# A decode step with attention and a gated MLP on one core: TensorE's middle as a loop, K transposed as 32-bit words, thin products with the activations stationary

## The chip, the cores and the metric

The kernel runs on one core of a Trainium2 chip. The metric is device time in microseconds, median of several executions. A profile of one execution stands beside the times; its span runs from the first to the last instruction and is a little shorter than the device time.

## The reference

```python
def reference(A_x, A_k_cache, A_v_cache, A_wq, A_wo, B_x, B_W_gate, B_W_up, B_W_down, gate_w):
    # x (4,1,512); caches (4,8,16384,128), the last W = 4096 rows count; 32 query heads, 4 per kv head
    q = (x @ wq) as (4, 32, 1, 128)
    p = softmax(q k^T * 128**-0.5);  o = p v
    a = o as (4, 1, 4096) @ wo
    gate = x @ W_gate;  up = x @ W_up                # 512 -> 1792
    b = (gate * (gate > 0) * up) @ W_down            # 1792 -> 512
    g = sigmoid((x * gate_w).sum(-1))
    return g * a + (1 - g) * b                       # x = A_x for both
```

All tensors are bf16. With 4 rows of activations the work is to bring in 81 MB: K and V 33.5 MB each, wq and wo 4.2 MB each, gate, up and down 1.8 MB each.

## The kernel before, in words

The 4 x 8 kv heads are taken four at a time, as eight **sets** `s` (`NSET`): one batch element and one half of its kv heads. A set's K is one 4 MB transfer into one half of `Ksb` (`load_k`, L158), its V the same into `Vsb` (`load_v`, L162); the two halves take turns. All big transfers are issued on SP's queue in one order: wq, K0, K1, V0, K2, V1, ..., K7, V6, gate, up, V7, down, wo in three pieces (`WO_CUTS`, L182). K of set `s` may be overwritten when the scores of `s` are done, V when its values are done. W_gate and W_up go into the first half of `Ksb`, W_down into that of `Vsb`, wo over wq in `Wbig`.

A list `Program` holds each engine's operations in an order written out by hand; `emit` turns named events into semaphore waits. Everything is unrolled. The phases of a set:

- `kt(s, i)`, i = 0..15 (L258): eight 128 x 128 bf16 transposes on PE (the piece of K stationary, `ident` moving) into one of three PSUM banks; one copy back into the same place of `Ksb`, nine on ACT (L263, `ACT_TAKES`), seven on DVE (L265).
- `scores(s, m)`, m = 0..7 (L280): four matmuls with `qT` stationary, side by side in four column groups of the array, 512 columns of transposed K moving; every second m a DVE instruction adds `mask` and takes the maximum (L290).
- `maximum`, `exponent`, `turn` (L297 to L326): the maximum over a head's keys, exp on ACT with row sums, a DVE transpose of the probabilities into `pT`.
- `values(s, k)`, k = 0..3 (L338): sixteen matmuls with `pT` stationary (32 columns), 256 columns of V moving, in four column groups; then a copy `osb`.
- `combine(s)` (L351, L354): eight fp32 matmuls with the selector `Wsel`, one with `Wsum`, a reciprocal and a product into `oq`.

PE's order interleaves transposes and scores of set `s` with the values of `s-1` and the combine of `s-2`. Ahead of set 0 stand the transpose of x (L226, fp32), the sigmoid gate and `qproj` (L366: 128 pairs, wq stationary, 4 columns of x moving). Behind set 7 stand `gateup` (L379: 112 pairs with W stationary, its columns read with a step of 14), the last values and combine, the down product (L444, 56 pairs) and wo (L452, 128 pairs), all with the weights stationary and 4 columns moving, into 16 columns of one bank; then a copy, a PE transpose, a copy and the output's transfer (L456 to L461).

Of the kernel before, what the change touches and what calls it, by code (L numbers as in the profile page):

```python
# [13 lines left out]
HQ = 32  # L14
# [5 lines left out]
NSET = 8  # L20
NFT = FF // 128
SCALE = DH ** -0.5
# [3 lines left out]
NTR = 3  # L26
NSC = 3
NPIECE = 2
NBANK = 4
WO_CUTS = (0, 16, 28, 32)  # L30
ACT_TAKES = (0, 1, 4, 6, 8, 9, 11, 13, 14)


class Program:

# [3 lines left out]
    def __init__(self):  # L39
        self.ops = {e: [] for e in self.ENGINES}  # L40
        self.events = {}
        self.counts = {e: 0 for e in self.ENGINES}
        self.dmas = []

    def op(self, engine, fn, name=None, waits=()):
        if name is not None:
            assert name not in self.events, name
            self.counts[engine] += 1
            self.events[name] = (engine, self.counts[engine])
        self.ops[engine].append((fn, name, tuple(waits), False))  # L50

    def dma(self, engine, fn, name, waits=()):
        assert name not in self.events, name
        sem = "d%d" % len(self.dmas)
        self.dmas.append(sem)
        self.events[name] = (sem, 16)
        self.ops[engine].append((fn, name, tuple(waits), True))

    def emit(self, engine, eng, sems):
        seen = {}  # L60
        for fn, name, waits, is_dma in self.ops[engine]:
            need = {}
            for w in waits:
                if w is None:
                    continue
                s, n = self.events[w]
                need[s] = max(need.get(s, 0), n)
            for s, n in need.items():
                if seen.get(s, 0) < n:
                    eng.wait_ge(sems[s], n)  # L70
                    seen[s] = n
            if fn is None:
                continue
            ins = fn(eng)
            if name is not None:
                s, _ = self.events[name]
                ins.then_inc(sems[s], 16 if is_dma else 1)


def bass_gated_mix__sliding_block_cached__glu_gated_reglu__decode_kernel(  # L80
# [13 lines left out]
    with ExitStack() as ctx:  # L94
# [7 lines left out]
        pT = sb("pT", [128, 2, 2048], BF16)  # L102
        mask = sb("mask", [128, 512], BF16)
        ident = sb("ident", [128, 128], BF16)
        ones = sb("ones", [128, 128], BF16)
# [6 lines left out]
        xT = sb("xT", [128, 32], BF16)  # L112
        xw = sb("xw", [5, 512], FP32)
        identf = sb("identf", [5, 8], FP32)
        gwB = sb("gwB", [128, 512], BF16)
        gsb = sb("gsb", [128, 8], FP32)
        qT = sb("qT", [128, NSET, 48], BF16)
# [12 lines left out]
        gtmp = sb("gtmp", [128, NFT * 4], FP32)  # L130
        gtmp2 = sb("gtmp2", [128, NFT * 4], FP32)
        hT = sb("hT", [128, NFT * 4], BF16)
        outT = sb("outT", [128, 16], BF16)
        out16 = sb("out16", [16, 128], BF16)
# [5 lines left out]

        Wg = Ksb[:, 0, 0:4 * FF].rearrange("p (t f) -> p t f", t=4)
# [7 lines left out]
        def trb(f):  # L149
            return TR[f % NTR][:].bitcast(BF16)  # L150

# [5 lines left out]
        def load_k(s):  # L157
            P.dma("sp", lambda e: e.dma_start(Ksb[:, s % 2, :], heads(A_k_cache, s)), ("K", s),  # L158
                  [("SC", s - 2, 2 * NBANK - 1)] if s >= 2 else [])

        def load_v(s):
            P.dma("sp", lambda e: e.dma_start(Vsb[:, s % 2, :], heads(A_v_cache, s)), ("V", s),  # L162
                  [("PV", s - 2, 3)] if s >= 2 else [])
# [3 lines left out]
        P.dma("sp", lambda e: e.dma_start(Wbig[:, :], A_wq.rearrange("(p t) w -> p (t w)", p=128)), ("WQ",))  # L167
        load_k(0)
        for s in range(1, NSET):
# [3 lines left out]
              ("WG",), [("SC", NSET - 2, 2 * NBANK - 1)])  # L173
        P.dma("sp", lambda e: e.dma_start(Ksb[:, 0, 4 * FF:8 * FF], B_W_up.rearrange("(p t) f -> p (t f)", p=128)),
              ("WU",), [("SC", NSET - 2, 2 * NBANK - 1)])
# [9 lines left out]
        P.op("pool", lambda e: e.memset(ones[:, :], 1.0), ("ONES",))  # L185
        P.op("pool", lambda e: e.affine_select(ident[:, :], ones[:, :], [[-1, 128]], ALU.is_equal, 0.0,
                                               base=0, channel_multiplier=1), ("IDENT",), [("ONES",)])
        P.op("pool", lambda e: e.memset(onesf[:, :], 1.0), ("ONESF",))
        P.op("pool", lambda e: e.memset(m4[:, :], -NEG), ("M4Z",))
        for a in range(4):  # L190
# [21 lines left out]
        P.op("dve", lambda e: e.memset(qT[:, :, :].rearrange("p s w -> p (s w)"), 0.0), ("QZ",))  # L212
# [4 lines left out]
        P.op("pool", lambda e: e.affine_select(identf[:, :], onesf[0:5, 0:8], [[-1, 8]], ALU.is_equal, 0.0,  # L217
                                               base=0, channel_multiplier=1), ("IDENTF",), [("ONESF",)])
        P.op("dve", lambda e: e.memset(xw[:, :], 0.0), ("XW0",))
        xwv = xw[:, :].bitcast(BF16).rearrange("r (k h) -> r k h", h=2)  # L220
        P.op("dve", lambda e: e.tensor_copy(xwv[:, :, 0:1], xsb[:, :].rearrange("r (k h) -> r k h", h=1)),  # L221
             ("XW",), [("XW0",), ("X",), ("GW",)])
        xv = xw[:, :].rearrange("r (p t) -> r t p", t=4)
        fbf = FB[:].bitcast(BF16).rearrange("p (k h) -> p k h", h=2)
        for t in range(4):
            P.op("pe", lambda e, t=t: e.transpose(FB[:, t * 8:t * 8 + 5], xv[0:5, t, :], identf[0:5, 0:5]),  # L226
                 ("XT",) if t == 3 else None, [("XW",), ("IDENTF",)])
        P.op("dve", lambda e: e.tensor_copy(xT[:, :].rearrange("p (t r) -> p t r", t=4)[:, :, 0:5],
                                            fbf[:, 0:32, 0].rearrange("p (t r) -> p t r", t=4)[:, :, 0:5]),
             ("XTC",), [("XT",)])  # L230
        P.op("dve", lambda e: e.tensor_copy(gwB[:, :].rearrange("p (t m) -> p t m", t=4),
                                            xT[:, :].rearrange("p (t r) -> p t r", t=4)[:, :, 4:5].to_broadcast([128, 4, 128])),
             ("GWB",), [("XTC",)])
        for t in range(4):
            P.op("pe", lambda e, t=t: e.matmul(FB[:, 32:36], gwB[:, t * 128:(t + 1) * 128], xT[:, t * 8:t * 8 + 4],
                                               start=(t == 0), stop=(t == 3)),
                 ("Z",) if t == 3 else None, [("GWB",)])
        P.op("act", lambda e: e.activation(gsb[:, 0:4], FB[:, 32:36], ACTF.Sigmoid), None, [("Z",)])
        P.op("act", lambda e: e.activation(gsb[:, 4:8], FB[:, 32:36], ACTF.Sigmoid, scale=-1.0), ("G",))
# [3 lines left out]
        tr_of = {}  # L243
# [4 lines left out]
        def kt(s, i):  # L248
            f = len(fills)
            fills.append((s, i))  # L250
            tr_of[(s, i)] = f
            bk = trb(f)
            for cc in range(8):
                c = 8 * i + cc
                w = []
                if cc == 0:
                    w = [("K", s), ("IDENT",)] + ([copy_done(f - NTR)] if f >= NTR else [])
                P.op("pe", lambda e, bk=bk, cc=cc, c=c, s=s: e.transpose(  # L258
                    bk[:, cc * 128:(cc + 1) * 128], Ksb[:, s % 2, c * 128:(c + 1) * 128], ident[:, :]),
                    ("KT", s, i) if cc == 7 else None, w)  # L260
            dst = Ksb[:, s % 2, i * 1024:(i + 1) * 1024]
            if i in ACT_TAKES:
                P.op("act", lambda e: e.activation(dst, bk[:, :], ACTF.Copy), ("KTC", s, i), [("KT", s, i)])  # L263
            else:
                P.op("dve", lambda e: e.tensor_copy(dst, bk[:, :]), ("KTC", s, i), [("KT", s, i)])  # L265

        def scores(s, m):
            bank, e2 = m // 2, m % 2
# [3 lines left out]
            lo = 16 * (1 - e2)  # L272
            k3 = Ksb[:, s % 2, :].rearrange("p (c k) -> p c k", k=128)
            for a in range(4):
                w = []
                if a == 0:
                    w = [("KTC", s, 2 * m), ("KTC", s, 2 * m + 1), ("QC",)]
                    if prev >= 0:
                        w.append(("SCC", prev // NBANK, prev % NBANK))
                P.op("pe", lambda e, a=a: e.matmul(  # L280
                    bk[32 * a:32 * a + 32, 0:512], qT[:, s, lo:lo + 32],
                    k3[:, 16 * m:16 * m + 16, 32 * a:32 * a + 32], start=(e2 == 0), stop=(e2 == 1),
                    tile_position=(0, 32 * a)),
                    ("SC", s, m) if a == 3 else None, w)
            if e2 == 0:
                return
            w = [("SC", s, m), ("MASK",)]
            if s >= 2 and bank == 0:
# [3 lines left out]
                mx[:, s % 2, bank:bank + 1]), ("SCC", s, bank), w)  # L292
# [31 lines left out]
        def turn(s, k):  # L324
            par = s % 2
            P.op("dve", lambda e: e.transpose(pT[:, par, k * PW:(k + 1) * PW], sc[:, par, k * PW:(k + 1) * PW]),  # L326
                 ("PTT", s, k), [("EXP", s, k), ("PV", s - 2, 3) if s >= 2 else None])

        def values(s, k):
            par = s % 2  # L330
            v4 = Vsb[:, par, :].rearrange("p (k g c d) -> p k c g d", k=4, g=2, d=128)
            for c in range(16):
                g = c % 4
                w = []
                if c == 0:
                    w = [("PTT", s, k * NPIECE // 4), ("V", s), ("OSB", s - 1) if s >= 1 else None]
                col = (16 * k + c) * 32
                P.op("pe", lambda e, c=c, g=g, col=col: e.matmul(  # L338
                    OB[32 * g:32 * g + 32, 0:256], pT[:, par, col:col + 32], v4[:, k, c, :, :],
                    start=(k == 0 and c < 4), stop=(k == 3 and c >= 12), tile_position=(0, 32 * g)),  # L340
                    ("PV", s, k) if c == 15 else None, w)
            if k == 3:
                P.op("dve", lambda e: e.tensor_copy(osb[:, par, :], OB[:, 0:256]), ("OSB", s),  # L343
                     [("PV", s, 3), ("SUMS", s - 2) if s >= 2 else None])

        def combine(s):
            par, b, half = s % 2, s // 2, s % 2
            r = slice(64 * half, 64 * half + 64)
            for k in range(8):
                lo = 3 - k % 4 + 64 * (k // 4)  # L350
                P.op("pe", lambda e, k=k, lo=lo: e.matmul(FB[r, 256:288], Wsel[:, lo:lo + 64], osb[:, par, 32 * k:32 * k + 32],  # L351
                                                          start=(k == 0), stop=(k == 7)), None,
                     [("OSB", s), ("WSUM",), ("QC",), ("G",), ("OQ", s - 1) if s >= 1 else None, ("H",) if s == NSET - 1 else None])
            P.op("pe", lambda e: e.matmul(FB[r, 288:288 + NPIECE], Wsum[:, :], rowsum[:, par, :], start=True, stop=True),  # L354
                 ("SUMS", s), [("EXP", s, NPIECE - 1)])
# [157 lines left out]
```

## Time and profile before

| | |
|---|---|
| device time, median of 3 runs | 200.47 us (200.23 to 200.69) |
| the profiled execution | span 198.9 us; of its device time nothing but this span is given |
| PE, PEld busy | 140.3 us, 110.7 us (2369 instructions each) |
| DVE, ACT, POOL busy | 101.5, 91.7, 5.5 us |
| read from HBM | 81.01 MB, mean 407 GB/s over the span |
| mean granted TensorE clock | 0.882 |

PE is the row of matmuls, PEld that of weight loads, which run beside them. Shares of busy time are averages over stages; the slices of the page, the windows and the timeline show a stage by itself. "L258" is line 258 of the kernel before.

### The profile page before, as it was taken

What the parts mean: (1) busy time and instruction counts of PE and PEld (TensorE: products, weight loads), DVE (VectorE), ACT (ScalarE), POOL (GpSimd) and SP (SyncE); (2) the same over time, 40 slices, a digit from 0 to 9 for tenths busy, and PEclk for the clock granted to TensorE, in tenths of its full rate; (3) what the DMA queues carried; (4) which work ended last, traced back from release to release, by engine and by line L of the source; (5) the groups of instructions that cost most, each with busy time, mean ns of one, the idle gap of its engine ahead of it and who ended that gap; (6) DMA issues with size and microseconds to landing.
All of it is one profiled execution on the core that took longest, in us unless ns stands there. A gap on an engine that the chain in (4) does not pass through costs nothing.

```text
span 198.9 us, 5220 instructions
## 1 busy us (share of the span) xinstructions
PE 140.3 (71%) x2369; PEld 110.7 (56%) x2369; DVE 101.5 (51%) x277; ACT 91.7 (46%) x108; POOL 5.5 (3%) x29
## 2 busy tenths in 40 slices
PE   0143199879789739983995299939994998179834
PEld 0133198547576438753773286738764865178733
DVE  1200034998688526854885168456845785611200
ACT  2000059698398318842972088507851883400000
POOL 7300000000000000000000000000000000000000
PEclk9999999999999957999999669975997899855755
DMA  6999999999999999999999999999999999999960
GB/s 225 435 442 458 435 428 422 419 422 420 445 435 432 428 432 430 432 428 419 422 425 435 438 435 428 420 428 425 428 432 435 419 406 437 459 398 419 419 258 7
DMA packets 3375, 81.33 MB, mean 409 GB/s; under 512 B 405, under 2 KB 410, under 8 KB 538
## 3 DMA queue, kind: packets, MB, share of 16 engines
q1 hardware_dynamic: 3344, 81.01, 95.4%
q8 instruction: 18, 0.29, 0.6%
q14 instruction: 3, 0.02, 0.0%
q10 hardware_dynamic: 10, 0.01, 0.0%
HBM read 81.01 MB, written 0.00 MB: 407 GB/s over the span
## 4 chain that ended last, share of the span: by engine, by line
DMA 59%; PE 30%; ACT 8%; issue 1%; SPq 1%; DVE 0%
DMA Ksb<-in_A_k_cache_dram 46%; PE bank L258 19%; DMA Wbig<-in_A_wo_dram 13%; ACT Ksb L263 6%; PE bank L280 6%; PE bank L338 3%; PE bank L351 2%; ACT sc L319 1%; PE bank L452 1%; ACT L319 1%; SPq L182 0%; SPq L167 0%; SPq L177 0%; PE bank L459 0%; PE bank L354 0%
## 5 line engine op out<-in xcount | busy, mean ns | idle before, releaser
L263 ACT ACTIVATE Ksb<-bank 128x1024 bf16<-128x1024 bf16 x72 | 71.0, 1023 | 67.8 <-PE bank L258 67.8
L258 PE MATMUL bank<-ident,Ksb 128*128 128x128 bf16 x1024 | 78.6, 238 | 30.2 <-DMA Ksb<-in_A_k_cache_dram 28.0
L258 PEld LDWEIGHTS bank<-ident,Ksb 128*128 128x128 bf16 x1024 | 66.9, 108 | 45.6 <-DMA Ksb<-in_A_k_cache_dram 29.8
L265 DVE COPY Ksb<-bank 128x1024 bf16<-128x1024 bf16 x56 | 38.2, 686 | 48.2 <-PE bank L258 47.9
L280 PE MATMUL bank<-Ksb,qT 128*32 128x512 bf16 x256 | 25.1, 398 | 3.5 <-ACT Ksb L263 2.4
L290 DVE CUSTOM_DVE_ANT_0 sc<-bank,mask 128x512 bf16<-128x512 f32 x32 | 21.5, 679 | 4.9 <-PE bank L280 4.1
L326 DVE STREAM_TRANSPOSE pT<-sc 128x1024 bf16<-128x1024 bf16 x16 | 19.7, 1234 | 2.9 <-ACT sc L319 2.9
L338 PE MATMUL bank<-Vsb,pT 128*32 128x256 bf16 x512 | 20.8, 291 | 0.0
L319 ACT ACTIVATE sc<-sc,negmax 128x1024 bf16<-128x1024 bf16 x16 | 18.3, 1144 | 4.6 <-DVE negmax L311 4.6
L338 PEld LDWEIGHTS bank<-Vsb,pT 128*32 128x32 bf16 x512 | 13.8, 102 | 3.8
L280 PEld LDWEIGHTS bank<-Ksb,qT 128*32 128x32 bf16 x256 | 6.6, 93 | 11.9 <-ACT Ksb L263 3.9
L379 PE MATMUL bank<-xT,Ksb 128*128 128x4 bf16 x112 | 6.9, 199 | 5.3 <-DVE oq L359 5.3
L351 PE MATMUL bank<-osb,Wsel 128*64 128x32 f32 x128 | 9.0, 225 | 1.2 <-DVE mq L297 0.7
L379 PEld LDWEIGHTS bank<-xT,Ksb 128*128 128x128 bf16 x112 | 6.8, 158 | 5.3 <-issue 5.3
L351 PEld LDWEIGHTS bank<-osb,Wsel 128*64 128x64 f32 x128 | 8.1, 139 | 2.7 <-DVE osb L343 1.0
L226 PE MATMUL bank<-identf,xw 5*128 5x5 f32 x4 | 0.6, 262 | 8.6 <-DVE xw L221 8.6
L452 PE MATMUL bank<-oq,Wbig 128*128 128x4 bf16 x128 | 3.7, 168 | 3.7 <-DMA Wbig<-in_A_wo_dram 3.7
L452 PEld LDWEIGHTS bank<-oq,Wbig 128*128 128x128 bf16 x128 | 3.6, 103 | 3.9 <-DMA Wbig<-in_A_wo_dram 3.9
L366 PE MATMUL bank<-xT,Wbig 128*128 128x4 bf16 x128 | 3.6, 166 | 2.9 <-DMA Wbig<-in_A_wq_dram 2.9
L226 PEld LDWEIGHTS bank<-identf,xw 5*128 5x128 f32 x4 | 0.6, 207 | 8.6 <-DVE xw L221 8.6
L311 DVE TENSOR_SCALAR negmax<-mall 32x1 f32<-32x1 f32 x32 | 4.6, 144 | 1.0
L366 PEld LDWEIGHTS bank<-xT,Wbig 128*128 128x128 bf16 x128 | 3.5, 104 | 3.0 <-DMA Wbig<-in_A_wq_dram 3.0
(53 smaller groups left out, 44.2 us busy)
## 6 DMA issues: line engine op xcount, KB each, us to landing
Ksb<-in_A_k_cache_dram SPq DMA_DIRECT2D x8, 4096.0 KB, 23.7
Vsb<-in_A_v_cache_dram SPq DMA_DIRECT2D x8, 4096.0 KB, 32.8
Wbig<-in_A_wq_dram SPq DMA_DIRECT2D x1, 4096.0 KB, 12.3
Wbig<-in_A_wo_dram SPq DMA_DIRECT2D x1, 2048.0 KB, 22.4
Ksb<-in_B_W_gate_dram SPq DMA_DIRECT2D x1, 1792.0 KB, 17.0
Ksb<-in_B_W_up_dram SPq DMA_DIRECT2D x1, 1792.0 KB, 20.9
Vsb<-in_B_W_down_dram SPq DMA_DIRECT2D x1, 1792.0 KB, 16.5
Wbig<-in_A_wo_dram SPq DMA_DIRECT2D x1, 1536.0 KB, 25.6
```

The lines of the kernel that those rows point to most:

```text
L258: P.op("pe", lambda e, bk=bk, cc=cc, c=c, s=s: e.transpose(bk[:, cc * 128:(cc + 1) * 128], Ksb[:, s % 2, c * 128:(c + 1) * 128], ident[:, :]),
L263: P.op("act", lambda e: e.activation(dst, bk[:, :], ACTF.Copy), ("KTC", s, i), [("KT", s, i)])
L265: P.op("dve", lambda e: e.tensor_copy(dst, bk[:, :]), ("KTC", s, i), [("KT", s, i)])
L280: P.op("pe", lambda e, a=a: e.matmul(bk[32 * a:32 * a + 32, 0:512], qT[:, s, lo:lo + 32], k3[:, 16 * m:16 * m + 16, 32 * a:32 * a + 32], s ...
L290: P.op("dve", lambda e: e.tensor_tensor_reduce(sc[:, s % 2, bank * 512:(bank + 1) * 512], bk[:, :], mask[:, :], 1.0, LOWEST, ALU.add, ALU.max,
L319: P.op("act", lambda e: e.activation(sc[:, par, k * PW:(k + 1) * PW], sc[:, par, k * PW:(k + 1) * PW], ACTF.Exp, bias=negmax[:, par:par + ...
L326: P.op("dve", lambda e: e.transpose(pT[:, par, k * PW:(k + 1) * PW], sc[:, par, k * PW:(k + 1) * PW]), ("PTT", s, k), [("EXP", s, k), ("PV ...
L338: P.op("pe", lambda e, c=c, g=g, col=col: e.matmul(OB[32 * g:32 * g + 32, 0:256], pT[:, par, col:col + 32], v4[:, k, c, :, :], start=(k == ...
L351: P.op("pe", lambda e, k=k, lo=lo: e.matmul(FB[r, 256:288], Wsel[:, lo:lo + 64], osb[:, par, 32 * k:32 * k + 32], start=(k == 0), stop=(k ...
L366: P.op("pe", lambda e, h=h, t=t: e.matmul(FB[:, 64 + 4 * h:68 + 4 * h], Wq3[:, t, 128 * h:128 * h + 128], xT[:, t * 8:t * 8 + 4], start=(t ...
L379: P.op("pe", lambda e, W=W, i=i, t=t, col=col: e.matmul(FB[:, col:col + 4], W[:, t, i:i + NFT * 127 + 1:NFT], xT[:, t * 8:t * 8 + 4], star ...
L452: P.op("pe", lambda e, i=i, cb=cb, last=last: e.matmul(AB[:, 4 * cb:4 * cb + 4], Wo3[:, i, cb * 128:(cb + 1) * 128], oq3[:, :, i], start=F ...
```

## The change

- **A loop on PE.** PE's operations of sets 2 to 7 are emitted once, as a loop of three turns with two sets each. `turn_edge` marks the edges, `signature` sees that all turns are alike. At the end of a turn PE drains and lowers the semaphores on which it waits within the turn, so that the next turn waits for the same counts. For this DVE, ACT and POOL count towards PE on semaphores of their own (`vd`, `va`, `pq`), K and V on one for each half, and `qS` holds a set's q in a place that depends on the set's parity alone. The other engines stay unrolled.
- **K as 32-bit words.** A transpose moves 128 x 128 words of two bf16 (`Kw`, `identw`): 64 instead of 128 a set, 16 copies of 512 words. Transposed K then has two neighbouring elements of the head beside each other; `scores` reads every second one (index `o`) against q ordered in the same way (`qW`). There are four transpose banks instead of three, two score banks instead of three.
- **Activations stationary.** q, gate and up take `xT` (32 columns, four used) as stationary operand and 512 or 448 columns of weights as moving, four column groups side by side; q is then copied and transposed with 16 small matmuls, the hidden row with a DVE transpose. down and wo take `hT` and `oq` (4 columns) as stationary, 128 columns moving in each of four column groups, and the sum stands in four rows of one bank, which two copies each on DVE and ACT take to `outr`.
- **wo's pieces** are rows 0 to 25, 26 to 29, and rows 30 and 31 in two halves of 256 columns; ahead of rows 0 to 25, of rows 26 to 29 and of the first half, four matmuls whose result is not used (`warm`) are emitted.
- **Ends.** wq's transfer is issued ahead of the block, the wait for the output's stands behind it.

```diff
-NTR = 3
-NSC = 3
+NTR = 4
+NSC = 2
-WO_CUTS = (0, 16, 28, 32)
+WO_CUTS = (0, 26, 30)
+LOOP_FIRST = 2
+LOOP_TURNS = 3
...
+        t = self.turns
+        self.emit_list(eng, sems, engine, ops[:t[0]], {}, {})
...
+        with eng.Fori(0, len(t) - 1):
+            self.emit_list(eng, sems, engine, ops[t[0]:t[1]], {}, {})
+            eng.drain()
+            for s, n in self.lowered.items():
+                eng.sem_inc(sems[s], -n)
+        shift = {s: (len(t) - 1) * n for s, n in self.lowered.items() if s not in self.shared}
+        self.emit_list(eng, sems, engine, ops[t[-1]:], shift, {})
...
+        Kw = Ksb[:, :, :].rearrange("p s w -> p (s w)").bitcast(FP32).rearrange("p (s w) -> p s w", s=2)
...
-        P.dma("sp", lambda e: e.dma_start(Wbig[:, :], A_wq.rearrange("(p t) w -> p (t w)", p=128)), ("WQ",))
...
+        wo_src3 = A_wo.rearrange("(p i) w -> p i w", p=128)
+        for u in range(2):
+            P.dma("sp", lambda e, u=u: e.dma_start(Wo3[:, WO_CUTS[-1]:32, 256 * u:256 * u + 256],
+                                                   wo_src3[:, WO_CUTS[-1]:32, 256 * u:256 * u + 256]), ("WOL", u), [("Q",)])
...
+        for half in range(2):
+            for t in range(4):
+                for g in range(4):
+                    col = 512 * (4 * half + g)
+                    P.op("pe", lambda e, half=half, t=t, g=g, col=col: e.matmul(
+                        SCB[half][32 * g:32 * g + 32, 0:512], xT[:, t, :], Wq3[:, t, col:col + 512],
+                        start=(t == 0), stop=(t == 3), tile_position=(0, 32 * g)),
...
+        for s in range(NSET):
+            P.op("pool", lambda e, s=s: e.tensor_copy(qS[:, s % 2, :, :], qW[:, s, :, :]), ("QS", s),
+                 [("QC", 0), ("QC", 1)] + ([("SC", s - 2, NBANK - 1)] if s >= 2 else []), sem="pq")
...
-            for cc in range(8):
-                c = 8 * i + cc
+            for cc in range(4):
+                c = 4 * i + cc
...
-                    bk[:, cc * 128:(cc + 1) * 128], Ksb[:, s % 2, c * 128:(c + 1) * 128], ident[:, :]),
-                    ("KT", s, i) if cc == 7 else None, w)
-            dst = Ksb[:, s % 2, i * 1024:(i + 1) * 1024]
+                    bk[:, cc * 128:(cc + 1) * 128], Kw[:, s % 2, c * 128:(c + 1) * 128], identw[:, :]),
+                    ("KT", s, i) if cc == 3 else None, w)
+            dst = Kw[:, s % 2, i * 512:(i + 1) * 512]
...
+            k4 = Ksb[:, s % 2, :].rearrange("p (c k o) -> p c k o", k=128, o=2)
+            for o in range(2):
+                for a in range(4):
...
+                        bk[32 * a:32 * a + 32, 0:512], qS[:, s % 2, o, :],
+                        k4[:, 16 * bank:16 * bank + 16, 32 * a:32 * a + 32, o], start=(o == 0), stop=(o == 1),
+                        tile_position=(0, 32 * a)),
...
+            for which, W, key in ((0, Wg, "WG"), (1, Wu, "WU")):
                 for t in range(4):
+                    for g in range(4):
+                        P.op("pe", lambda e, which=which, W=W, t=t, g=g: e.matmul(
+                            TR[which][32 * g:32 * g + 32, 0:FQ], xT[:, t, :], W[:, t, FQ * g:FQ * g + FQ],
+                            start=(t == 0), stop=(t == 3), tile_position=(0, 32 * g)),
...
+        def product(stat, mov, cb, start, stop, name, waits):
+            P.op("pe", lambda e: e.matmul(AB[32 * cb:32 * cb + 4, 0:128], stat, mov[:, 128 * cb:128 * cb + 128],
+                                          start=start, stop=stop, tile_position=(0, 32 * cb)), name, waits)
+
+        def warm(n):
+            for k in range(n):
+                P.op("pe", lambda e: e.matmul(SCB[1][:, 0:256], ident[:, :], mask[:, 0:256], start=True, stop=True),
+                     None, [("MASK",), ("SCC", NSET - 1, NBANK - 1), ("SCC", NSET - 1, 1)])
...
         for k in range(len(WO_CUTS) - 1):
+            warm(4)
             for i in range(WO_CUTS[k], WO_CUTS[k + 1]):
                 for cb in range(4):
+                    product(oq3[:, :, i], Wo3[:, i, :], cb, False, False, None, [("WO", k), ("OQ", NSET - 1)])
+        warm(4)
+        for u in range(2):
+            for i in range(WO_CUTS[-1], 32):
+                for cb in (2 * u, 2 * u + 1):
+                    product(oq3[:, :, i], Wo3[:, i, :], cb, False, i == 31,
+                            ("ACC", u) if (i == 31 and cb == 2 * u + 1) else None, [("WOL", u)])
+        for u in range(2):
+            for cb, eng in ((2 * u, "dve"), (2 * u + 1, "act")):
...
+                P.op(eng, fn, ("FIN", cb), [("ACC", u)], sem="fin")
...
+        nc.sync.dma_start(Wbig[:, :], A_wq.rearrange("(p t) w -> p (t w)", p=128)).then_inc(sems["wq"], 16)
         with nc.Block() as block:
             @block.sync
             def _(e):
                 P.emit("sp", e, sems)
+                e.wait_ge(sems["fin"], 4)
+                e.dma_start(out.rearrange("b o d -> (b o) d"), outr[:, :]).then_inc(sems["done"], 16)
...
+        nc.sync.wait_ge(sems["done"], 16)
```

More of the change, by code (lines that the diff above doesn't have):

```diff
@@ L21 @@
 NFT = FF // 128
+FQ = FF // 4
 SCALE = DH ** -0.5
@@ new lines, in turn_edge, with need @@
+    def turn_edge(self):
+        self.turns.append(len(self.ops["pe"]))
+    def need(self, engine, waits):
+        need = {}
+        for w in waits:
+            if w is None:
+                continue
+            s, n, by, at = self.events[w]
+            for own, mine in (("dve", "vd"), ("act", "va")):
+                want = mine if engine == "pe" else own
+                if by == own and s in (own, mine) and s != want:
+                    s = want
+                    n = 1 + sum(1 for k in self.history[s] if k < at)
+                    assert n <= self.counts[s], w
+            need[s] = max(need.get(s, 0), n)
+        return need
@@ L70, in emit, with per_turn, emit_list @@
+    def per_turn(self):
+        return self.lowered
+    def emit_list(self, eng, sems, engine, ops, shift, seen):
+        for fn, name, waits, is_dma in ops:
+            for s, n in self.need(engine, waits).items():
+                n -= shift.get(s, 0)
+                if n > 0 and seen.get(s, 0) < n:
                     eng.wait_ge(sems[s], n)
@@ new lines, in bass_gated_mix__sliding_block_cached__glu_gated_reglu__decode_kernel @@
+        for half in range(2):
+            src = SCB[half][:, :].rearrange("p (h w o) -> p h o w", h=4, o=2)
+            for cc in range(2):
+                dst = qrow[:, half, :].rearrange("p (h o c w) -> p h o c w", h=4, o=2, c=2)[:, :, :, cc, :]
+                which = [("Q",) if half else ("QH",)]
+                if half == 0:
+                    P.op("dve", lambda e, src=src, dst=dst: e.tensor_copy(dst, src), ("QR", half, cc), which, sem="vd")
+                else:
+                    P.op("act", lambda e, src=src, dst=dst: e.copy(dst, src), ("QR", half, cc), which, sem="va")
```

301 lines of the change are left out of this document (161 added, 140 removed).

## The prediction

> **What bounds the kernel now.** I read the page first: shares of the engines, the slices, the queues.
>
> ```profile
> span 198.9 us, 5220 instructions
> PE 140.3 (71%) x2369; PEld 110.7 (56%) x2369; DVE 101.5 (51%) x277; ACT 91.7 (46%) x108; POOL 5.5 (3%) x29
> DMA  6999999999999999999999999999999999999960
> GB/s 225 435 442 458 435 428 422 419 422 420 445 435 432 428 432 430 432 428 419 422 425 435 438 435 428 420 428 425 428 432 435 419 406 437 459 398 419 419 258 7
> q1 hardware_dynamic: 3344, 81.01, 95.4%
> q8 instruction: 18, 0.29, 0.6%
> ```
>
> No engine is full, but the DMA row is, from the second slice to the thirty-eighth, at some 430 GB/s. The kernel is a stream of 81 MB; the rest either hides behind it or stands at its two ends. The q8 row is the second thing to see: 18 packets of 16 KB are instructions, 0.6% of 16 engines' 198.9 us, or 1.06 us each on one engine. Of 2369 + 2369 PE instructions that is one packet for every 263, so I take these to be PE's code.
>
> Next the windows view around the end of the stream (columns: stretch, length, busy time of PE, PEld, DVE, ACT, POOL, clock, DMA share, GB/s).
>
> ```profile
> 60.00:70.00 10.00, 7.96 (x152) 5.50 (x148) 7.03 (x21) 5.39 (x6) 0.00 (x0) 1.00 1.00 426
> 190.00:190.50 0.50, 0.00 (x0) 0.00 (x0) 0.00 (x0) 0.00 (x0) 0.00 (x0) 0.50 0.85 352
> 190.50:191.00 0.50, 0.27 (x10) 0.28 (x11) 0.00 (x0) 0.00 (x0) 0.00 (x0) 0.50 0.54 229
> 193.00:193.50 0.50, 0.00 (x0) 0.00 (x0) 0.00 (x0) 0.00 (x0) 0.00 (x0) 0.50 0.57 213
> 193.50:194.00 0.50, 0.00 (x0) 0.00 (x0) 0.00 (x0) 0.00 (x0) 0.00 (x0) 0.50 0.08 33
> 194.50:195.00 0.50, 0.50 (x23) 0.50 (x23) 0.00 (x0) 0.00 (x0) 0.00 (x0) 0.50 0.08 33
> 195.00:195.50 0.50, 0.50 (x25) 0.50 (x23) 0.00 (x0) 0.00 (x0) 0.00 (x0) 0.50 0.00 0
> ```
>
> The stream doesn't end at once. At about 190.45 us half of the 16 engines fall silent; the other half works on until 193.5; one stays until 195.0. All carry the same share of the data, so the late ones did something else meanwhile. I read it as the 18 code packets shared by eight engines: two each make them 3.0 us late, or 1.5 us a packet (1.06 of it the packet itself), and the two packets left over make the last stretch of 1.5 us. The eight that end early are not sped up by their neighbours' lateness: 229 GB/s at a share of 0.54 is the same 424 per whole share as 426 at 1.00. So **without code packets the stream would end near 190.5**.
>
> The timeline shows what follows the stream, and when the second last big transfer was issued.
>
> ```profile
> 167.93 0.33 SPq L177 DMA_DIRECT2D Vsb<-in_B_W_down_dram  x1
> 190.73 1.87 PE L452 MATMUL bank<-oq,Wbig 128*128 128x4 bf16 x64 [1.96 <-DMA Wbig<-in_A_wo_dram]
> 194.38 1.87 PE L452 MATMUL bank<-oq,Wbig 128*128 128x4 bf16 x64 [1.78 <-DMA Wbig<-in_A_wo_dram]
> 196.29 0.20 DVE L456 CAST outT<-bank 128x16 bf16<-128x16 f32 x1 [8.25 <-PE bank L452]
> 196.54 0.27 PE L459 MATMUL bank<-ident,outT 128*16 128x128 bf16 x1 [0.29 <-DVE outT L456]
> 196.85 0.21 DVE L460 COPY out<-bank 16x128 bf16<-16x128 bf16 x1 [0.36 <-PE bank L459]
> 197.09 0.36 SPq L461 DMA_DIRECT2D out_dram<-out  x1
> ```
>
> From 195.0 to 198.9 stand 3.9 us: products until 196.25, a copy, a transpose and a copy until 197.06, and 1.8 for the output transfer and the end.
>
> **The change, part by part.** First PE in the middle of the stream, where it must only keep up: a row of the view of waits (us in total, times, longest), five of the timeline, and one of the page's groups.
>
> ```profile
> PE bank L258 <- DMA Ksb<-in_A_k_cache_dram: 28.0, 7, 7.5
> 79.47 1.07 PE L258 MATMUL bank<-ident,Ksb 128*128 128x128 bf16 x16
> 8.62 0.64 PE L226 MATMUL bank<-identf,xw 5*128 5x5 f32 x4 [8.62 <-DVE xw L221]
> 78.00 1.12 PE L351 MATMUL bank<-osb,Wsel 128*64 128x32 f32 x16
> 79.14 0.40 PE L280 MATMUL bank<-Ksb,qT 128*32 128x512 bf16 x4
> 181.86 3.61 PE L338 MATMUL bank<-Vsb,pT 128*32 128x256 bf16 x64
> L263 ACT ACTIVATE Ksb<-bank 128x1024 bf16<-128x1024 bf16 x72 | 71.0, 1023 | 67.8 <-PE bank L258 67.8
> ```
>
> PE waits seven times for K, 28.0 us, 4.0 a set. *Transposes:* a set has 128 now, at 1.07/16 = 67 ns, 8.6 us. After, 64 of 32-bit words. The nearest row is L226, 32-bit transposes with 128 stationary columns but five moving ones: 0.64/4 = 160 ns with the last one's tail. The combine's 32-bit matmuls take 1.12/16 = 70 ns at 64 stationary columns, 140 at 128. Eight such matmuls per combine stand as 16 instructions, but four 32-bit transposes as four, so a transpose is not split as a matmul is. I take 140 ns: 64 x 140 = 9.0 us, 0.4 more; from below 67 (a gain of 4.3), from above 250 (four times the row of today, a loss of 7.4, a rival below). *Scores:* 32 matmuls as before, now with every second bf16 as moving data; no row shows this stride. Eight groups at 0.40 make 3.2 us; doubled they cost 3.2 more. Together at most 3.6 on the value I take for transposes, under the 4.0 of waiting. *Copies* hold 512 words for 1024 halves; ACT's 1023 ns should not grow, and its longest waits are for PE. *q* (128 matmuls to 32 and 16 small ones, four copies) lies between the landings of wq and the first K, where PE idles over 7 us (the longest of the seven waits). *gate and up* (112 to 32) wait for data long before the end. The *drain and seven decrements* of a turn fall where PE waits 4.0 us for K. All of this I cost at nothing, covered by the stream.
>
> *Code.* I count the PE instructions after, two per matmul and two for each half of a 32-bit matmul. Ahead of the loop 312 matmuls (8 for x, 48 for q, 96 for set 0, 160 for set 1); a turn has two sets of 64 + 32 + 64 + 18 = 178; behind it 328 (combine twice 18, gate and up 32, values 64, down 56, wo 128, warm 12). Stored are 2 x (312 + 356 + 328) = 1992 instructions, against 4738; executed 3416. At 263 a packet: 7.6 packets if the loop's body, fetched once, is kept over its turns, 13.0 if each pass is fetched again. I take the first: eight packets over eight engines is one each, so the stream ends at 190.45 + 1.5 = 191.95 instead of 195.0.
>
> *The start.* wq is issued ahead of the block. It leaves at most the step from SP's release to its issue, under 0.1 us; I take 0.05 earlier. *Last pieces:* 0.26 MB in runs of 512 bytes; between 0 and 0.6 us (twice their time at 430 GB/s), I take 0.2. Stream end: **192.1**.
>
> *The tail.* The first wo piece is now 26 of 32 rows, so it lands 6/32 of 4.19 MB = 0.79 MB, or 1.8 us, before the end: 190.3. Then come 104 pairs. L452 has 29 ns a pair; L338, four side by side with 256 columns, 56 ns at the low clock, or 28 for half the columns, and half of that, 14, at the full clock. I take 25: 2.6 us, to 192.9, past the stream's end. So PE, not the stream, ends last there. Four warm matmuls of 256 columns: twice 67 ns each, 0.5 us (cold, alone, 4 x 56 = 224 ns each, 0.9), to 193.4; 16 pairs, 0.4, 193.8; warm again, 0.5, 194.3; 8 pairs, 0.2, 194.5; copies of 128 columns side by side on DVE and ACT, 0.3 (0.20 for 16 columns now), 194.8. The transpose and one copy are gone. The output's 1.8 us lose the barrier of the block's end, which now runs beside the transfer; I take 0.3: 194.8 + 1.5 = **196.3**.
>
> Against the profiled 198.9 that is 2.6 less. The three runs' median, 200.47, lies 1.6 above this span; I leave that 1.6 as it is and forecast **197.9 us**. The unknowns of the sum are -1.4 to +0.5 (pairs), +0.8 (warm), -0.2 to +0.4 (runs): 196.3 to 199.6 in this case.
>
> **The rivals.** *No code packets at all*, since all 1992 instructions stay from the run before. Then the stream ends at 190.6: 196.4 us. Against it: the present program fetches 18 packets for 18.0 times 263 instructions, as if nothing stayed.
>
> *Every pass is fetched, and each branch waits.* Thirteen packets and one more for each of two taken branches make 15, two each on most of eight engines: stream end 193.6, time 199.4. The wait at a branch, a packet's 1.06 us and perhaps the 1.4 us that a small transfer takes (the output's), lies in the K waits of 4.0. Should the count reach 17, one engine has three: 200.9, and the gain is gone. In the Trainium skill, the page "Runtime: NRT & Kernel Launch", section "Instruction fetch mechanics", speaks for this case and against the loop: a taken branch whose target isn't in the two 16 KB pages at hand waits for a fetch. The same section gives PE a store of 2048 instructions, by which the loop would fit. The trace decides neither, as it has no branch back; I leave both cases a chance.
>
> *PE becomes the bound (slower).* The place is the set's 64 transposes. They may cost 8.6 + 4.0 = 12.6 us before PE falls behind the stream: 197 ns each. At 250 ns they take 16.0, 3.4 over, six sets 20 us. W_down's load waits for the values of set 6 (issued at 167.93), and from there to the end stand 27 us for 6.0 MB that need 14, so 13 are hidden: +7 us on the forecast, 205, and more where the stride of the scores costs too. For it: 160 ns in L226 includes hardly any moving columns. Against it: transposes aren't split. In the Trainium skill, "TensorE: Matmul & The Clock Gate", section "Terms", calls the transpose mode four times faster for FP32; no run here shows that yet.
>
> **How the numbers follow.** The forecast 0.50; no packets 0.12; fetched again, two each, 0.18; three on an engine 0.07; PE bound 0.13. The range leaves out the last two, 0.20: from 196.0 (no packets, pairs at 22 ns) to 200.2 (two each with the dear tail). A measurement of this kernel tells 0.2%, 0.4 us, from no change. Faster by more: 0.50 + 0.12 + 0.16 = 0.78. Within: 0.02 of two each and 0.03 of three, 0.05. Slower: 0.04 and 0.13, 0.17.
>
> **What would show it.** The queue row of instructions with 8 packets or fewer, against 13 to 17; the DMA share falling to a half near 190.4 and to nothing before 192.5; PE's K waits still near 4 us a set, and transposes under 197 ns; the last products ending behind the stream by 2 us or so, and the output's issue near 194.9. I am wrong if the stream breaks in the middle (GB/s under 420 over several slices), or if the engines' late ends have another cause than code, so that they stay at 195 with few packets.

## The result, and the profile after

| | before | after |
|---|---|---|
| device time, median of 9 runs each | 200.63 us (200.23 to 200.88) | 199.63 us (198.92 to 200.28) |
| ratio | | 0.9949, 95% interval 0.9933 to 0.9965 |
| profiled execution: span | 198.9 us | 198.4 us |
| time outside the span (device time less span) | 1.76 us (median of 23 runs of before) | 1.2 to 1.4 us |

The change saves 1.0 us, where 2.6 were forecast. The page after:

```profile
span 198.4 us, 3970 instructions
PE 138.5 (70%) x1708; PEld 105.3 (53%) x1708; DVE 105.3 (53%) x282; ACT 63.8 (32%) x112; POOL 7.3 (4%) x37
GB/s 225 456 449 436 436 423 426 423 423 415 436 443 453 423 426 424 429 439 429 423 423 423 436 456 424 429 423 429 443 436 429 409 406 461 423 419 458 398 199 4
q8 instruction: 8, 0.13, 0.3%
```

The stream runs as fast as before, and the instruction packets are 8 instead of 18. The windows view at the stream's end (same columns as in the prediction):

```profile
190.50:191.00 0.50, 0.00 (x0) 0.00 (x0) 0.00 (x0) 0.00 (x0) 0.00 (x0) 0.50 0.66 257
192.00:192.50 0.50, 0.50 (x32) 0.50 (x24) 0.00 (x0) 0.00 (x0) 0.00 (x0) 0.50 0.16 47
192.50:193.00 0.50, 0.50 (x28) 0.50 (x20) 0.00 (x0) 0.00 (x0) 0.00 (x0) 0.50 0.00 0
```

The stream falls silent between 192.0 and 192.5 (its last data packet ends at 192.47), not at 195.0 as before. In the records of landings, wo's last piece is complete at 192.91, against 195.58 before: 2.7 us earlier. The timeline shows where these 2.7 us went:

```profile
191.01 2.95 PE L543 MATMUL bank<-Wbig,oq 128*4 128x128 bf16 x104 [5.13 <-DMA Wbig<-in_A_wo_dram]
193.89 1.03 PE L548 MATMUL bank<-mask,ident 128*128 128x256 bf16 x4
194.86 0.60 PE L543 MATMUL bank<-Wbig,oq 128*4 128x128 bf16 x16
195.39 0.80 PE L548 MATMUL bank<-mask,ident 128*128 128x256 bf16 x4
196.12 0.29 PE L543 MATMUL bank<-Wbig,oq 128*4 128x128 bf16 x8
196.44 0.60 DVE L568 CAST outr<-bank 4x128 bf16<-4x128 f32 x2 [11.57 <-PE bank L543]
197.06 0.35 SPq L594 DMA_DIRECT2D out_dram<-outr  x1
```

From 191.01 PE is busy without a break: the 104 pairs of wo's big first piece, four warm matmuls, 16 pairs, four warm ones, eight pairs. The last product ends at 196.41, 3.5 us behind the last landing; before, it ended 0.7 us behind it (196.25). The balance against before, in the two profiled executions: stream's end -2.7, from there to the last product +2.8, copies -0.2, output within the span -0.45, and -0.5 outside it.

### The profile page after: what moved, and what is told of

It is laid out like the page before. It is cut to its first block, busy times and chain, and to the rows that moved or that the text cites. A ratio compares the mean times of both kernels' runs of the same rounds, so it can differ in the third digit from the quotient of the medians.

```text
span 198.4 us, 3970 instructions
## 1 busy us (share of the span) xinstructions
PE 138.5 (70%) x1708; PEld 105.3 (53%) x1708; DVE 105.3 (53%) x282; ACT 63.8 (32%) x112; POOL 7.3 (4%) x37
## 4 chain that ended last, share of the span: by engine, by line
DMA 58%; PE 34%; DVE 5%; issue 1%; SPq 0%; ACT 0%; DVEq 0%
DMA Ksb<-in_A_k_cache_dram 46%; PE bank L366 21%; DMA Wbig<-in_A_wo_dram 12%; PE bank L387 5%; DVE Ksb L373 3%; PE bank L442 2%; PE bank L543 2%; PE bank L456 2%; PE bank L548 1%; DVE sc L395 1%; DVE pT L431 1%; DVE mq L402 0%; ACT Ksb L371 0%; DVE negmax L416 0%; SPq L588 0%
## 5 line engine op out<-in xcount | busy, mean ns | idle before, releaser
L366 PE MATMUL bank<-identw,Ksb 128*128 128x128 f32 x512 | 79.4, 318 | 26.5 <-DMA Ksb<-in_A_k_cache_dram 26.5
L366 PEld LDWEIGHTS bank<-identw,Ksb 128*128 128x128 f32 x512 | 70.0, 166 | 36.1 <-DMA Ksb<-in_A_k_cache_dram 28.3
L371 ACT COPY Ksb<-bank 128x512 f32<-128x512 f32 x72 | 41.2, 586 | 87.6 <-PE bank L366 87.5
L373 DVE COPY Ksb<-bank 128x512 f32<-128x512 f32 x56 | 37.6, 685 | 43.7 <-PE bank L366 43.5
L387 PE MATMUL bank<-Ksb,qS 128*32 128x512 bf16 x256 | 20.2, 391 | 4.3 <-DVE Ksb L373 4.1
L387 PEld LDWEIGHTS bank<-Ksb,qS 128*32 128x32 bf16 x256 | 4.2, 95 | 11.5 <-DVE Ksb L373 6.5
L543 PE MATMUL bank<-Wbig,oq 128*4 128x128 bf16 x128 | 3.8, 303 | 5.1 <-DMA Wbig<-in_A_wo_dram 5.1
L448 DVE COPY osb<-bank 128x256 f32<-128x256 f32 x8 | 3.4, 420 | 6.7 <-PE bank L442 6.7
L543 PEld LDWEIGHTS bank<-Wbig,oq 128*4 128x4 bf16 x128 | 3.1, 120 | 6.0 <-DMA Wbig<-in_A_wo_dram 5.4
L316 PE MATMUL bank<-Wbig,xT 128*32 128x512 bf16 x32 | 3.6, 631 | 3.0 <-DMA Wbig<-in_A_wq_dram 3.0
```

The costliest lines, as they stand in the source:

```text
L316: P.op("pe", lambda e, half=half, t=t, g=g, col=col: e.matmul(SCB[half][32 * g:32 * g + 32, 0:512], xT[:, t, :], Wq3[:, t, col:col + 512], ...
L366: P.op("pe", lambda e, bk=bk, cc=cc, c=c, s=s: e.transpose(bk[:, cc * 128:(cc + 1) * 128], Kw[:, s % 2, c * 128:(c + 1) * 128], identw[:, :]),
L371: P.op("act", lambda e: e.copy(dst, bk[:, :]), ("KTC", s, i), [("KT", s, i)], sem="va")
L387: P.op("pe", lambda e, a=a, o=o: e.matmul(bk[32 * a:32 * a + 32, 0:512], qS[:, s % 2, o, :], k4[:, 16 * bank:16 * bank + 16, 32 * a:32 * a ...
L543: P.op("pe", lambda e: e.matmul(AB[32 * cb:32 * cb + 4, 0:128], stat, mov[:, 128 * cb:128 * cb + 128], start=start, stop=stop, tile_positi ...
```

## The experiments

The theory behind them all: the stream ends earlier because it carries fewer instruction packets, and PE's backlog behind it takes the gain back. Ratios are to the kernel before, timed in the same round. Its median was 200.47 to 200.63 us in the different rounds, so a difference between two changed kernels of different rounds is known to some 0.2 us.

**The warm matmuls left out.**

```diff
-            for k in range(n):
+            for k in range(0):
```

> The changed kernel without its twelve warm matmuls. Theory A (the gain of an earlier stream is spent on products behind the stream, which PE works off one after the other): the second and third group of warm matmuls stand on the path with 0.96 and 0.73 us, so the last product ends 1.7 us earlier, at 194.7, and the span falls from 198.4 to about 196.7; instruction packets stay 8, the last landing of wo stays near 192.9. Rival B (they only fill time in which PE waits for wo, or keep its clock up): no change, or slower, with pairs dearer than 28 ns.

197.88 us (ratio 0.9858, 0.984 to 0.9877), span 196.6. The timeline:

```profile
191.02 3.59 PE L543 MATMUL bank<-Wbig,oq 128*4 128x128 bf16 x128 [5.75 <-DMA Wbig<-in_A_wo_dram]
195.27 0.35 SPq L594 DMA_DIRECT2D out_dram<-outr  x1
```

All 128 pairs run through from the same landing, the output is issued 1.8 us earlier, and the last landing stays (192.9). So the second and third group of warm matmuls stood on the path, as theory A said.

**wo cut once more.**

```diff
-WO_CUTS = (0, 26, 30)
+WO_CUTS = (0, 16, 26, 30)
```

> The changed kernel with wo cut at rows 16, 26 and 30 instead of 26 and 30; the warm matmuls stay (16 of them). Theory A: 64 of the 104 pairs are done before row 26 has landed at 191.0, the other 40 take 1.1 us, and the last product ends 1.8 us earlier, near 194.6; span 196.6. Rival B (the transfers' landings set the end, PE follows them): the last landing stays at 192.9 and the end within 0.3 us of 198.4. Rival C (one more transfer on the queue costs as much as it saves): the last landing moves behind 193.5.

197.65 us (0.9837, 0.9806 to 0.9868), 2.0 less than the change. In the profiled run the last product ended at 195.2, 1.2 us earlier than in the change, and the last landing was 193.1. This is theory A, though by less than the 1.8 us expected: the pairs behind row 16 began 0.2 us late, and the last warm group, at a clock of 0.50, took 1.04 us where it took 0.80 in the change. The six runs fell in two groups, 196.7 to 197.0 and 198.3 to 198.5; the profiled one is of the slower. More on that below.

**Both repairs.**

> The changed kernel with both repairs of the tail: wo cut at rows 16, 26 and 30, and no warm matmuls. Theory A (the end is PE's backlog behind landings of 191.0, 192.2, 192.6 and 192.9): 40 pairs from 191.1 end at 192.3, 16 more at 192.8, the last eight follow the last landing and end near 193.3; copies 0.6, output 1.35: span 195.3, 3.1 less than the changed kernel, device time near 196.5. Rival B (without backlog another wait takes its place): less than 2.2 off the changed kernel's span.

```profile
188.00 1.27 PE L543 MATMUL bank<-Wbig,oq 128*4 128x128 bf16 x64 [2.95 <-DMA Wbig<-in_A_wo_dram]
191.14 2.33 PE L543 MATMUL bank<-Wbig,oq 128*4 128x128 bf16 x64 [1.86 <-DMA Wbig<-in_A_wo_dram]
193.23 0.54 ACT L570 CAST outr<-bank 4x128 bf16<-4x128 f32 x2 [22.03 <-PE bank L543]
193.85 0.35 SPq L594 DMA_DIRECT2D out_dram<-outr  x1
```

196.69 us (0.9821, 0.9804 to 0.9838), span 195.2: as expected, and 2.9 us under the change (2.8 when each is taken against the kernel before of its own round). Half the pairs are done before row 26 lands, and the copies start at 193.23, 0.2 us after the last landing (193.0). It is the fastest version here.

**PE's loop written out.**

```diff
+        self.emit_list(eng, sems, engine, ops, {}, {})
+        return
         t = self.turns
         self.emit_list(eng, sems, engine, ops[:t[0]], {}, {})
...
         def loop_sem(kind, s):
+            return None
...
-        for s in ("K0", "K1", "V0", "V1"):
-            per[s] = 16
-            P.shared[s] = True
```

> The changed kernel with PE's loop written out, each K and V transfer on a semaphore of its own; all else the same. Theory A (every 256 instructions that PE runs through for the first time cost one instruction packet, and each packet makes one DMA engine 1.5 us late): some 3420 instructions give 13 packets instead of 8, two on several engines, the last landing of wo goes from 192.9 to about 194.4, the span from 198.4 to 199.9. Rival B (the engines' late ends have another cause): the last landing stays at 192.9. Rival C (the loop's drains and branches cost more than its packets save): faster than the changed kernel.

> The same with PE's loop written out: tail repaired, 13 instruction packets instead of 8. Theory A (the loop's worth is the stream's end alone, so it is the same whatever the tail): 1.1 to 1.5 us above the kernel with both repairs, last landing 194.2 against 192.9. Rival B (the loop's worth came with the backlog): the same time as with the loop.

The first expectation is of the change with the loop written out, the second of the same with both repairs of the tail.

The change with the loop written out takes 200.72 us (1.0008, 0.9993 to 1.0023): its whole gain is gone. Of its page and windows:

```profile
q8 instruction: 13, 0.21, 0.4%
192.00:192.50 0.50, 0.20 (x12) 0.21 (x16) 0.00 (x0) 0.00 (x0) 0.00 (x0) 0.50 0.38 142
193.50:194.00 0.50, 0.50 (x32) 0.50 (x24) 0.00 (x0) 0.00 (x0) 0.00 (x0) 0.50 0.26 60
```

At 193.5 four engines still work (0.26 of 16); the last landing is 194.2. With the repaired tail the loop written out costs the same: 197.73 us (0.9864, 0.9849 to 0.9878) against 196.69, 1.0 more, last landing 194.4 against 193.0. The loop is worth 1.0 to 1.1 us, a little under the 1.1 to 1.5 expected, as an earlier end of the stream. The other half of the stream's gain was there without the loop: with 13 packets for 18 the last landing moved from 195.6 to 194.2, with 8 for 13 to 192.9. The first step goes with the smaller number of PE instructions (3416 for 4738); no run separates the parts of the change that bring it.

The records of landings show the mechanism step by step. Each big transfer lands in 16 parts, which I take to be one of each engine. The table gives, for some transfers, when the first part landed, how many instruction packets had begun by then, how many parts came more than 0.85 us behind the first ("one step"), more than 2.7 ("two") and more than 4.5 ("three"), and by how much the last part came behind the first. The last row is wo's last piece.

```text
           before                      loop written out            after
landing    packets 1/2/3 steps last    packets 1/2/3 steps last    packets 1/2/3 steps last
 12.6 us      0     0 0 0      +0.5       0     0 0 0      +0.6       0     0 0 0      +0.6
 61           4     5 0 0      +2.0       2     3 0 0      +1.9       2     3 0 0      +2.0
 90           7     8 0 0      +2.0       5     7 0 0      +1.9       5     6 0 0      +2.0
129          11     9 3 0      +3.4       8    10 0 0      +2.1       5     6 0 0      +2.2
148.6        13     9 5 0      +3.5       9    10 1 0      +3.4       5     6 0 0      +2.2
181          16     9 8 0      +3.5      11    10 3 0      +3.5       5     6 0 0      +2.2
190.8        17     9 8 1      +4.8      12     9 4 0      +3.3       7     8 0 0      +2.1
```

Each packet puts one more engine behind, for good. The first eight fall on eight engines, the ninth lifts one of them to two steps (the row 148.6 of the loop written out), the seventeenth one to three (the last row of before). The records give the lags and not the engines' names, so that the packets go round the eight in turn is read from these counts. One or two more engines lag with no packet of this queue; why is not known. The change's loop has no packet from 87.5 to 182.4 us: two returns to the loop's start fetch nothing. The branch that returns took 0.21 to 0.24 us, a turn's end with drain (1.0), decrements (0.15 apart) and branch 2.4 us.

**One packet more, then two.** 128 pairs of 4 columns without use, where PE idles ahead of the first K; in the second kernel 128 more behind gate and up.

```diff
+        for _ in range(128):
+            P.op("pe", lambda e: e.matmul(TR[0][:, 0:4], ident[:, :], mask[:, 0:4], start=True, stop=True), None,
+                 [("MASK",), ("IDENT",)])
... (the second kernel, behind gateup())
+        for _ in range(128):
+            P.op("pe", lambda e: e.matmul(TR[2][:, 0:4], ident[:, :], mask[:, 0:4], start=True, stop=True))
```

> The changed kernel with 128 pairs of 4 columns without use ahead of the first transposes, where PE waits for the first K for 4.7 us and they need 3.6: 256 instructions more, one packet more, no more work on the path. Theory A (packets go round eight engines, so the ninth falls on one that is late already): the last landing goes from 192.9 to 194.2 to 194.4, the time up by 1.2 to 1.5 us. Rival B (lateness grows in proportion to the packets, 2.7 us for ten in the change): up by 0.3.

> The kernel with 128 pairs ahead of the first transposes (e8_nine) and 128 more behind gate and up, where PE waits 7.6 us for the last V: two packets more than in the changed kernel, nine of them ahead of the stream's end instead of seven. Theory A (eight engines take the packets in turn, and each packet makes its engine 1.3 to 1.5 us late for good): the eighth packet cost nothing in e8_nine, the ninth is the first to meet an engine that is late already; the last landing goes from 193.2 to 194.3 or so, the device time from 199.4 to 200.5. Rival B (0.3 us a packet, in proportion): last landing 193.5, time 199.7.

With nine packets the time is 199.41 us (0.9941, 0.9928 to 0.9953), no slower than the change; the last landing is 193.2. My expectation had counted wrongly: the last packet comes when the stream is over (195.0; in the change 194.3), so eight of nine count, one for each engine. The run decides nothing between the theories; the 0.3 us by which the last landing moved is even what rival B said. With ten, nine of them ahead of the end, it is 200.83 us (1.0011, 0.9998 to 1.0025), 1.4 more for the one packet; the last landing is 194.2, and a single engine is two steps behind. Rival B had 193.5 and 199.7. Of its page and windows:

```profile
q8 instruction: 10, 0.16, 0.3%
192.50:193.00 0.50, 0.50 (x26) 0.50 (x23) 0.00 (x0) 0.00 (x0) 0.00 (x0) 0.50 0.09 33
193.50:194.00 0.50, 0.50 (x32) 0.50 (x24) 0.00 (x0) 0.00 (x0) 0.00 (x0) 0.50 0.04 11
```

That one engine (one of 16 is a share of 0.06; its last data packet ends at 193.78) holds wo's first piece back: its pairs start at 192.40, against 191.28 with nine packets and 191.01 in the change. The stream's end goes by the worst engine, not in proportion to the packets.

**The wait for the output.** Back inside the block in the kernel after; behind the block in the kernel before. Shown is the edit of the second.

```diff
-        P.op("sp", None, None, [("OUT",)])
...
+        nc.sync.wait_ge(sems[P.events[("OUT",)][0]], 16)
```

> The changed kernel with the wait for the output's transfer inside the block again. Theory A (the block's end beside the output's transfer saves 0.2 us of the span, and the time outside the span falls because the other engines leave early, from 1.8 before to 1.2): span plus 0.2 to 0.3, time outside the span back to 1.7, device time plus 0.7. Rival B (the difference outside the span is chance): time outside the span stays 1.2, device time plus 0.2 to 0.3.

> The kernel before with one part of the change alone: the wait for the output's transfer stands behind the block. Theory A (it brings the time outside the span from 1.76 to 1.25 whatever the rest): device time 0.5 to 0.7 less, 200.0, 18 instruction packets as before. Rival B (the smaller time outside the span belongs to the shorter program): no change.

After with the wait inside: 200.39 us (0.999, 0.9976 to 1.0004), outside the span 1.68 to 1.85 us in its twelve runs. Before with the wait outside: 199.59 us (0.9958, 0.9945 to 0.997), outside 1.24 to 1.37, span 198.4, still 18 packets. Both ways it is 0.8 to 0.9 us, of which 0.5 lie outside the span; that is more than the 0.5 to 0.7 expected for the kernel before. This one line by itself gives almost the whole gain of the change. The rest of it nets 0.1 to 0.2, which the run with the wait inside (interval up to 1.0004) can't tell from nothing.

**More work on PE in the middle.** 21 matmuls of 256 columns without use in each set of the loop.

> The changed kernel with 21 matmuls of 256 columns without use in each set of the loop, ahead of its eleventh group of transposes: 2.6 us of PE's work more a set at the full clock, 42 x 2 instructions more in the stored body, none more outside it. Theory A (PE's middle is covered by the stream, with K waits of 3.5 to 4.9 us a set): the waits for K shrink to 1 to 2 us, device time the same within 0.4 of 199.6. Rival B (PE's middle sets the stream's pace through the order in which K and V come free): 2 us a set comes through in part, 201 or more.

Of its waits and its timeline:

```profile
PE bank L369 <- DMA Ksb<-in_A_k_cache_dram: 17.9, 5, 4.7
PE bank L369 <- PEq L138: 3.9, 2, 2.0
193.83 0.61 PE L551 MATMUL bank<-mask,ident 128*128 128x256 bf16 x4
194.37 0.40 PE L546 MATMUL bank<-Wbig,oq 128*4 128x128 bf16 x16
```

199.17 us (0.9936, 0.9924 to 0.9949): no slower. The waits for K fall from 26.5 to 17.9 us, less than I expected, and at two turns the loop's own end becomes what PE waits for, 2.0 us each: that is its price, which the wait for K hides in the change. PE's middle doesn't set the time. That it was 0.5 us faster goes with the tail, the last two rows: the second warm group took 0.61 us, not 1.03, and the 16 pairs 0.40, not 0.60.

**What stays open.** Most kernels with warm matmuls scatter by 1.3 to 1.8 us (the change 1.4, with the additional cut 1.8, with ten packets 1.5; with more work in the middle only 0.8), and those without by less (0.6; with both repairs and the loop written out 0.25; with both repairs alone four runs within 0.31, and a fifth with an unusual 2.45 us outside its span). They also had fewer runs.

In the profiled executions the length of the tail goes with the granted clock. Six traces have the same tail, with the change's cuts and warm matmuls: the change, the loop written out, nine and ten packets, the wait inside, more work in the middle. In them the clock rises from 0.50 to 1.00 between 2.8 and 5.5 us behind the start of wo's pairs, and the later it rises, the later the last product ends, in the same order in all six: 4.6 us behind the start with more work (rise at 2.8), 5.4 in the change (4.8), 5.7 with nine packets (5.5). Four warm matmuls take 1.03 us at 0.50 and 0.61 at 1.00. In the three traces without warm matmuls the clock stays at 0.50 to the end, and so it does in that of the additional cut, whose run was of the slower group. So I take the moment at which the clock rises to be the cause of the scatter in the other runs too; no run isolates it.

## Why the prediction was right or wrong

Forecast were 2.6 us less, measured were 1.0. The step that failed is the tail: the sum took 4.2 us from the stream's end (192.1) to the end of the span (196.3), and the run took 5.9 (192.5 to 198.4), because the landing came later behind the stream's end, PE's work behind it was dearer, and there were more copies than costed.

**The bound and the mechanism: right.** The stream is the bound up to its end, and code packets make eight of its engines late. Forecast were 7.6 packets with the loop's body kept, stream end 192.1; measured were 8, end 192.5, last landing 192.9. The eight engines, read from the share of 0.54, and the steps of 1.5 us (1.3 to 1.5) are borne out by the landings. One reading was off without harm: the last stretch of before, 193.5 to 195.0, is one engine with the seventeenth packet, not two packets left over; the eighteenth began only at 193.5 and put no further engine behind. The rival with no packets at all fell, and so did the one that fetches every turn again. The Trainium skill's rule, in "Runtime: NRT & Kernel Launch", "Instruction fetch mechanics", that a branch out of the two pages at hand waits for a fetch, does not hold for this loop: a turn is 712 instructions, near three packets, and its two returns fetched nothing.

**PE in the middle: right.** The waits for K stayed (26.5 us for 28.0). A 32-bit transpose costs, by the timeline of two stretches, 1.97/16 = 123 ns at the full clock and 4.51/24 = 188 where the clock stood at 0.50 for the first 3.5 of the 4.5 us; I took 140. The price of 250 ns did not occur. Scores didn't grow with the stride: 391 ns an instruction, 398 before (L280).

```profile
159.70 1.97 PE L366 MATMUL bank<-identw,Ksb 128*128 128x128 f32 x16
72.83 4.51 PE L366 MATMUL bank<-identw,Ksb 128*128 128x128 f32 x24 [3.15 <-DMA Ksb<-in_A_k_cache_dram]
L387 PE MATMUL bank<-Ksb,qS 128*32 128x512 bf16 x256 | 20.2, 391 | 4.3 <-DVE Ksb L373 4.1
```

**The tail: the terms that were mis-sized.** That PE would end behind the stream was in the sum, and so were its steps; nearly each came out dearer, all in one direction:

| step | forecast | measured |
|---|---|---|
| wo's first piece lands | 190.3 | 191.0 |
| 104 pairs | 2.6 | 2.9 |
| warm, second group | 0.5 | 1.0 |
| 16 pairs | 0.4 | 0.5 |
| warm, third group | 0.5 | 0.7 |
| 8 pairs | 0.2 | 0.3 |
| copies, to the output's issue | 0.3 | 0.65 |
| output, within the span | 1.5 | 1.3 |

Together +2.1 us on the span. Of the first row, 0.4 is the time between the last packet (192.47) and the landing's record (192.91), which I hadn't added, and the rest the stream's end itself, 192.5 for 192.1. For the pairs and the warm matmuls I took values near the full clock, though the rows of that stretch stand at a clock of 0.50. The prices at that clock were in the working as the dear side, 29 ns a pair (L452) and 224 ns for 256 columns, and they came close: 28 ns for each of the 104 pairs, 240 for each matmul of the second warm group. For the copies I had counted one on each engine; there are two. The pairs (+0.5) and the warm matmuls (+0.7) stayed within the unknowns that the sum names; the landing (+0.7) and the copies (+0.35) had no place there. The warm matmuls themselves were the avoidable part: without them (1.8 us less) and with the additional cut the stream's gain comes through, 196.69 us. The sign that I had named, the output's issue near 194.9, failed with this step: it was 197.06.

**The time outside the span: not seen.** I carried 1.6 us over unchanged; it was 1.76 and fell to 1.2 with the moved wait. Inside the span the move gave 0.3 to 0.4 us (from the output's issue to the end 1.34 us against 1.68 with the wait inside, and 1.38 against 1.81 in the kernel before), near the 0.3 that I had costed. So the forecast of 197.9 missed by +2.1 in the tail and -0.4 outside the span. That the second made up for part of the first is luck, and so is it that 199.63 lies within my range: its upper end, 200.2, was drawn for a loop that is fetched again, which did not occur.

## What to carry to other kernels

Where a stream of transfers is the bound, the last of its engines ends it: look at the share of busy DMA engines at the end, and count what else they carried. Here PE's instructions were a load on these engines; a loop or fewer instructions paid off by steps, when the last packet was taken from the worst engine. Behind such an end, price each instruction at the clock that the profile shows there, cut the last transfers so that little work is left when the last one lands, and put nothing without use in between.

## What the runs showed of the hardware that was not expected

- An instruction packet of 16 KB (1.06 us) makes its DMA engine 1.3 to 1.5 us late for the rest of the execution; by the counts of late landings, eight of the 16 engines take them in turn.
- A PE loop of 712 instructions came back to its start with no instruction packet and a branch of 0.21 to 0.24 us; its drain took 1.0 us, and the decrements of semaphores stand 0.15 apart.
- The wait for the last transfer, behind the block instead of in it, saves 0.8 to 0.9 us here, 0.5 of them outside the span.
- The clock granted to PE rose from 0.50 to 1.00 at another moment of the tail in each of six traces of the same tail (2.8 to 5.5 us behind its start); four matmuls of 256 columns took 1.03 us before it and 0.61 behind it.
